# Second MLP's up-projections in seven products for eight, passes of 768 tokens, weights by way of DRAM; first MLP in 8+8 chunks

## The chip, the cores and the metric

One core of one Trainium2 chip. The metric is the device time of one execution in microseconds (us); lower is better. The time of the kernel before is the median of three runs. Executions differ by about 0.1% around it.

## The reference

A decayed linear attention on 2304 tokens (4 x 576), then two MLPs on its output. What matters here are the MLPs, with d_model 512:

```python
h = np.maximum(x @ w_in, 0.0)          # first MLP, d_ff 2048
x = h * h @ w_out
a, b = x @ w_a, x @ w_b                # second MLP, d_ff 1536
out = a * b @ w_out2
```

Inputs are float32 here; the weights arrive as float64 (pairs of 32-bit words) and are turned into float32 on the chip.

## The kernel before, in words

All matmuls of the MLPs work on float32 values split in two: a high part rounded to `fp32r` (ACT cast) and the remainder (DVE subtraction, `sub`, L236). A product is three matmuls: high weight x high data, low weight x high data, high weight x low data. `mm` (L227) issues each of them, so all matmuls of the kernel have that one line in the trace; the tiles tell them apart: `bank<-x,w` is an up-projection, `bank<-gh,w` a down-projection, `qkr`, `pt`, `tv` belong to attention.

The 2304 tokens are four `BLOCKS` of 512 and one of 256. d_ff is cut into chunks of 128: 16 in the first MLP, 12 in the second. `GROUPS` says which chunks are taken together: for each group all five blocks are run, and the group's sums over its chunks lie in banks 0 to 3 until the group's last chunk (`evac_y` L643 then copies or adds them to `yt` or `xt` in SBUF). `up(i)` (L670) issues one chunk and block: for each of `ph` weights (1 in the first MLP, 2 in the second) 4 x 3 matmuls into one of the `hbanks` (bank 7 alone until attention is over, then banks 4 to 7), then the element-wise step: Relu (L699) and Square (L713) on ACT in the first group, a copy (L699) and a product on DVE (L704, L708) in the others; then the split into `gh`. `down(i)` (L724) issues its 4 x 3 matmuls, written after the next chunk's `up`. `split_x` (L618) splits a block's input into four `x` slots.

A weight piece (512 columns) is loaded by `w_load` (L323): a transfer of 512 KB of float64 words into a `raw` buffer, ACT operations (L344, L370), four DVE operations (L348, L355, L363, L374) that put the float32 together in a `wf` buffer, then the split into a slot `w` of `wslot` by an ACT cast and a DVE subtraction. `pump` (L386) does that when a slot comes free. The first 16 pieces are loaded during attention. When attention and its buffers are done, `enter` (L761) gives their space to `yt`, three raw buffers and three more slots.

Nothing runs in the written order as such: every step goes to `Plan.add` with its engines, its cost and the buffers it reads and writes; `Plan.order` (L101) gives each step a latest start, taken back from the sequence of PE's work, and then plays through the engines, each taking the ready step with the earliest latest start. The order it finds is emitted, and each engine and the one transfer queue (SP) work it off in that order.

Of the kernel before, what the change touches and what calls it, by code (L numbers as in the profile page):

```python
# [44 lines left out]
WF, WE, RAWS = 4, 2, 3  # L45
SLOTS = dict(
    x=4, g=2, r=2, gh=2, qkr=3, vr=3, tv=2, pt=2, sa=2, wraw=4, ys=4,
# [162 lines left out]
def tile_retention_two_mlps(  # L210
# [36 lines left out]
    big = ctx.enter_context(tc.tile_pool(name="big", bufs=1))  # L247
    dram = ctx.enter_context(tc.tile_pool(name="dram", bufs=1, space=bass.MemoryType.DRAM))
    psum = ctx.enter_context(tc.tile_pool(name="psum", bufs=1, space=PSUM))

    xt = [big.tile([P, KT, n], F32, name=f"xt{t}") for t, (_, n) in enumerate(BLOCKS)]
# [16 lines left out]
    ring(big, "x", [P, 2, 512], F32R, SLOTS["x"])  # L268
# [3 lines left out]
    wslot = [big.tile([P, 2, 512], F32R, name=f"w{i}") for i in range(NW0)] + [None] * (NW - NW0)  # L272
# [4 lines left out]
    ap = st.enter_context(tc.tile_pool(name="attn", bufs=1))  # L277
# [28 lines left out]
    todo = [(ph, c, j) for ph, g in GROUPS for c in g for j in range(ph + 1)]  # L306
    wt = {}
    used = {}
    state_ = {"next": 0, "n": NW0, "entered": None, "loads": 0}
    raws = []  # L310

# [11 lines left out]
    def w_load(ph, c, j, i):  # L323

        w, kw = slot("wf")
        rest, ke = slot("we")
        src = (w1 if ph == 1 else w2)[c, :, j, :]
        parts = [("w", i, 0), ("w", i, 1)]
        ex = [state_["entered"]] if i >= NW0 else []
        wu = w.bitcast(U32)  # L330
# [12 lines left out]
        plan.add(  # L343
            {"ACT": act(512)}, lambda e: A.activation(w, hi().bitcast(F32), AF.Abs), [kraw], [kw]  # L344
        )
        plan.add(
            {"DVE": dve2(512)},
            lambda e: V.tensor_scalar(  # L348
                out=w, in0=w, scalar1=F64_MIN, scalar2=F64_MAX, op0=ALU.max, op1=ALU.min
            ),  # L350
            w=[kw],
        )
        plan.add(
            {"DVE": dve2(512)},
            lambda e: V.tensor_scalar(  # L355
                out=wu, in0=wu, scalar1=3, scalar2=0x3FFFFFF8,
                op0=ALU.logical_shift_left, op1=ALU.bitwise_and,
            ),
            w=[kw],
        )  # L360
        plan.add(
            {"DVE": dve(512)},
            lambda e: V.scalar_tensor_tensor(  # L363
                out=wu, in0=hi(), scalar=0xC0000000, in1=wu, op0=ALU.bitwise_and, op1=ALU.bitwise_or
            ),
            [kraw], [kw],
        )
# [4 lines left out]
        plan.add(  # L372
            {"DVE": dve(512)},
            lambda e: V._custom_dve(  # L374
                ADD32_U16LIMBS, out=w.bitcast(U16), in0=w.bitcast(U16), in1=rest.bitcast(U16)
            ),
            [ke], [kw],
        )
        plan.add({"ACT": act(512)}, copy(lambda: wslot[i][:, 0, :], lambda: w), [kw], parts[:1], ex)
        plan.add(  # L380
            {"DVE": dve(512), "POOL": pool(512)},
            sub(lambda: wslot[i][:, 1, :], lambda: w, lambda: wslot[i][:, 0, :]),
            [kw, parts[0]], parts[1:], ex,
        )

    def pump():  # L386
        while todo:
            i = state_["next"] % state_["n"]
            if i in used.values():
                return  # L390
            used[todo[0]] = i
            wt[todo[0]] = i
            state_["next"] = i + 1
            w_load(*todo.pop(0), i)
# [243 lines left out]
    for gi, (ph, g) in enumerate(GROUPS):  # L638
        for bi, t in enumerate(ORDERS[gi]):
            for ci, c in enumerate(g):  # L640
                seq.append((gi, ph, t, c, ci == 0, ci == len(g) - 1, bi == len(BLOCKS) - 1))

    def evac_y(gi, t, m):  # L643
        c0, n = BLOCKS[t]
        ph = GROUPS[gi][0]
# [11 lines left out]
        kd = tokens("yt" if ph == 1 else "xt", m, c0, n)  # L657

        def d():
            return yt[0][:, m, c0:c0 + n] if ph == 1 else xt[t][:, m, :]  # L660

        ex = [state_["entered"]]
        if gi == 0 or ph == 2 and GROUPS[gi - 1][0] == 1:
# [3 lines left out]
        if gi == len(GROUPS) - 1:  # L667
            plan.add(dmac(P * 4 * n), dma(lambda: out[:, m, c0:c0 + n], d), kd)

    def up(i):  # L670
        gi, ph, t, c, first, last, lastb = seq[i]
# [6 lines left out]
        for j in range(ph):  # L678
            b = hbanks[0][hbanks[1] % len(hbanks[0])]
            hbanks[1] += 1  # L680
            o, ko = bank[b], ("bank", b)
            wi = wt[ph, c, j]
            for k in range(KT):
                x, kx = xs[gi, t, k]

                def f(e, k=k, x=x, wi=wi, o=o):
                    w = wslot[wi]
                    cs = slice(k * P, (k + 1) * P)
                    mm(o[:, :n], w[:, 0, cs], x[:, 0, :n], k == 0, False)
                    mm(o[:, :n], w[:, 1, cs], x[:, 0, :n], False, False)  # L690
                    mm(o[:, :n], w[:, 0, cs], x[:, 1, :n], False, k == KT - 1)

                plan.add(mmc(n, n, n), f, [("w", wi, 0), ("w", wi, 1), kx, kx + (1,)], [ko])
                yield t
            if j == 0:
                fn = AF.Relu if ph == 1 else AF.Copy
                plan.add(
                    {"ACT": act(n, True)},
                    lambda e, o=o: A.activation(r[:, :n], o[:, :n], fn), [ko], [kr],  # L699
                )  # L700

        def prod(e):
            if ph == 1:
                V.scalar_tensor_tensor(  # L704
                    out=g[:, :n], in0=o[:, :n], scalar=0.0, in1=r[:, :n], op0=ALU.max, op1=ALU.mult
                )
            else:
                V.tensor_mul(g[:, :n], o[:, :n], r[:, :n])  # L708

        if gi == 0:  # L710

            for to, key in ((lambda: gh[:, 0, :n], kgh), (lambda: g[:, :n], kg)):
                plan.add({"ACT": act(n)}, lambda e, to=to: A.activation(to(), r[:, :n], AF.Square), [kr], [key])  # L713
        else:
            plan.add({"DVE": dve(n)}, prod, [ko, kr], [kg])
            plan.add({"ACT": act(n)}, copy(lambda: gh[:, 0, :n], lambda: g[:, :n]), [kg], [kgh])
        plan.add(
            {"DVE": dve(n), "POOL": pool(n)},
            sub(lambda: gh[:, 1, :n], lambda: g[:, :n], lambda: gh[:, 0, :n]),
            [kg, kgh], [kgh + (1,)],  # L720
        )
        return gh, kgh

    def down(i, gh, kgh):  # L724
        gi, ph, t, c, first, last, lastb = seq[i]
        n = BLOCKS[t][1]
        wi = wt[ph, c, ph]

        def f(e, ms, which):
            for m in ms:  # L730
                a, w, cs = bank[m][:, :n], wslot[wi], slice(m * P, (m + 1) * P)
                if 0 in which:
                    mm(a, w[:, 0, cs], gh[:, 0, :n], first, False)
# [5 lines left out]
        if last:  # L739
            for m in range(KT):  # L740
# [4 lines left out]
                evac_y(gi, t, m)  # L745
                yield t
        else:
            for h in range(2):
                for m in range(KT):
# [4 lines left out]
                    if m % 2 or h == 0:  # L754
                        yield t
        if lastb:
            for j in range(ph + 1):
                used.pop((ph, c, j))
            pump()

    def enter():  # L761
# [3 lines left out]
        def swap(e):  # L765
            st.close()
            late = ctx.enter_context(tc.tile_pool(name="late", bufs=1))
            yt[0] = late.tile([P, KT, NT], F32, name="yt")
            raws.extend(late.tile([P, 1024], U32, name=f"raw{i}") for i in range(RAWS))
            for i in range(NW0, NW):  # L770
                wslot[i] = late.tile([P, 2, 512], F32R, name=f"w{i}")
# [10 lines left out]
        state_["n"] = NW  # L782
        state_["next"] = NW0
        pump()

    rings_a = ["qkr", "vr", "tv", "pt", "wraw", "vt", "gt", "mask", "md", "sp", "sa", "ys"]

    def mlps():
        prev = None
        for i in range(len(seq)):  # L790
            gi, ph, t, c, first, last, lastb = seq[i]
# [9 lines left out]
        yield from down(len(seq) - 1, *prev)  # L801

# [6 lines left out]
    for t in mlps():  # L809
# [5 lines left out]
        before = plan.pe  # L815
    steps, total = plan.order()
# [72 lines left out]
```

## Time and profile before

| | |
|---|---|
| median of three runs | 907.05 us (906.63 to 907.87) |
| span of the profiled execution | 906.5 us |
| PE, PEld, DVE, ACT busy | 98%, 83%, 54%, 42% of the span |
| bytes moved | 66.12 MB, mean 73 GB/s |

The profile is of one execution, whose own time is not listed apart from the span; the span runs from its first to its last instruction. PE is TensorE's matmuls, PEld its weight loads, DVE is VectorE, ACT ScalarE, SP the engine that issues transfers. Matmuls overlap, so the time from the start of one group to the start of another tells more than a single duration. DVE and ACT durations contain an end that overlaps the next instruction.

### The profile page before, as it was taken

The page shows a single profiled execution, that of the slowest core. Times are in us where ns is not written, and L with a number is a line of the kernel's source. Part 1 is how long each engine was busy: PE and PEld are TensorE (multiplying, and loading weights), DVE is VectorE, ACT ScalarE, POOL GpSimd, SP SyncE. Part 2 cuts the span into 40 slices and gives each one's busy share as a digit, 9 for nine tenths or more (in the row PEclk, how much of TensorE's full clock was granted, in tenths as well). Part 3 has the DMA queues.
Part 4 walks back from the last instruction along what each step waited for, and adds up shares of the span by engine and source line. Part 5 has one row for each costly group of instructions (what it writes and reads, how often), then busy time and mean ns, then how long its engine had stood idle before and what let it go on. Part 6 is the DMA issues. An engine that isn't in the chain of part 4 may idle for free.

```text
span 906.5 us, 14973 instructions
## 1 busy us (share of the span) xinstructions
PE 891.6 (98%) x6256; PEld 755.4 (83%) x6256; DVE 492.1 (54%) x978; ACT 381.6 (42%) x703; POOL 0.7 (0%) x6
## 2 busy tenths in 40 slices
PE   5999999999999999999999999999999999999998
PEld 5787888888998889888888888898888898888888
DVE  6999544137699747964595213299332253322323
ACT  3676334346786536643464223276222132221221
POOL 0000000000000000000000000000000000000000
PEclk9999999999999999999999999999999999999999
DMA  8884531027343300310032000034000000011101
GB/s 271 296 275 123 177 105 48 1 56 259 129 138 106 103 1 24 117 47 1 1 117 70 1 1 1 1 96 138 0 1 1 1 1 1 9 38 47 46 2 71
DMA packets 22100, 66.12 MB, mean 73 GB/s; under 512 B 2448, under 2 KB 3088, under 8 KB 22032
## 3 DMA queue, kind: packets, MB, share of 16 engines
q1 hardware_dynamic: 21888, 65.15, 22.1%
q8 instruction: 49, 0.80, 0.4%
q14 instruction: 19, 0.16, 0.1%
q10 hardware_dynamic: 144, 0.01, 0.0%
HBM read 57.28 MB, written 7.86 MB: 72 GB/s over the span
## 4 chain that ended last, share of the span: by engine, by line
PE 94%; DVE 4%; DMA 1%; issue 1%; ACT 0%; SPq 0%; DVEq 0%; ACTq 0%
PE bank L227 94%; DMA vr<-vk 1%; DVE wf L374 1%; DVE wf L363 1%; DVE w L236 1%; DMA vt<-vtab 0%; DVE pt L567 0%; DVE sa L589 0%; DVE wf L348 0%; DVE xt L552 0%; DVE wf L355 0%; DVE gh L236 0%; ACT tv L477 0%; DVE xt L239 0%; ACT r L699 0%
## 5 line engine op out<-in xcount | busy, mean ns | idle before, releaser
L227 PE MATMUL bank<-x,w 128*128 128x512 f32 (+1 forms) x2400 | 535.9, 369 | 1.8 <-ACT r L699 0.7
L227 PEld LDWEIGHTS bank<-x,w 128*128 128x128 f32 x2400 | 420.4, 188 | 78.0 <-ACT r L699 1.1
L227 PE MATMUL bank<-gh,w 128*128 128x512 f32 (+1 forms) x1680 | 386.8, 369 | 0.4 <-DVE w L236 0.4
L227 PEld LDWEIGHTS bank<-gh,w 128*128 128x128 f32 x1680 | 296.0, 189 | 54.1 <-DVE w L236 1.1
L699 ACT ACTIVATE r<-bank 128x512 f32<-128x512 f32 (+1 forms) x140 | 77.6, 555 | 320.4 <-PE bank L227 320.0
L708 DVE TENSOR_TENSOR g<-bank,r 128x512 f32<-128x512 f32 (+1 forms) x60 | 38.3, 638 | 180.2 <-PE bank L227 179.3
L236 DVE TENSOR_TENSOR gh<-g,gh 128x512 fp32r<-128x512 f32 (+1 forms) x140 | 88.9, 635 | 70.1 <-ACT g L713 45.2
L233 ACT CAST gh<-g 128x512 fp32r<-128x512 f32 (+1 forms) x100 | 58.0, 580 | 110.9 <-DVE g L708 94.7
L236 DVE TENSOR_TENSOR x<-yt,x 128x512 fp32r<-128x512 f32 (+1 forms) x60 | 36.0, 634 | 50.2 <-ACT x L233 50.1
L233 ACT CAST w<-wf 128x512 fp32r<-128x512 f32 x68 | 41.7, 618 | 22.3 <-DVE wf L374 19.6
L236 DVE TENSOR_TENSOR w<-wf,w 128x512 fp32r<-128x512 f32 x68 | 46.4, 686 | 8.5 <-ACT w L233 8.0
L374 DVE CUSTOM_DVE_ANT_0 wf<-wf,we 128x1024 uint16<-128x1024 uint16 x68 | 46.4, 685 | 0.5
L236 DVE TENSOR_TENSOR x<-xt,x 128x512 fp32r<-128x512 f32 (+1 forms) x60 | 37.2, 635 | 12.2 <-ACT x L233 9.2
L704 DVE SCALAR_TENSOR_TENSOR g<-bank,r 128x512 f32<-128x512 f32 (+1 forms) x40 | 25.4, 636 | 30.5 <-ACT r L699 30.2
L370 ACT ACTIVATE we<-raw 128x512 int32<-128x512 uint32 x52 | 34.7, 671 | 14.5 <-DVE wf L374 14.1
L233 ACT CAST x<-xt 128x512 fp32r<-128x512 f32 (+1 forms) x60 | 33.8, 577 | 15.8 <-PE bank L227 15.3
L344 ACT ACTIVATE wf<-raw 128x512 f32<-128x512 f32 x52 | 34.4, 671 | 5.7 <-DMA raw<-w 5.1
L233 ACT CAST x<-yt 128x512 fp32r<-128x512 f32 (+1 forms) x60 | 33.4, 577 | 4.9 <-PE bank L227 4.0
L363 DVE SCALAR_TENSOR_TENSOR wf<-raw,wf 128x512 uint32<-128x512 uint32 x52 | 35.3, 685 | 0.2
L348 DVE TENSOR_SCALAR wf<-wf 128x512 f32<-128x512 f32 x68 | 28.1, 421 | 3.2 <-ACT wf L344 2.6
L239 DVE TENSOR_TENSOR yt<-bank,yt 128x512 f32<-128x512 f32 (+1 forms) x40 | 23.3, 630 | 11.3 <-PE bank L227 11.3
L355 DVE TENSOR_SCALAR wf<-wf 128x512 uint32<-128x512 uint32 x68 | 28.1, 421 | 0.2
(42 smaller groups left out, 367.9 us busy)
## 6 DMA issues: line engine op xcount, KB each, us to landing
raw<-w SPq DMA_DIRECT2D x52, 512.0 KB, 3.7
vr<-vk SPq DMA_DIRECT2D x16, 448.0 KB, 4.2
qkr<-qk SPq DMA_DIRECT2D x16, 448.0 KB, 4.8
wraw<-w SPq DMA_DIRECT2D x12, 512.0 KB, 6.6
out<-xt SPq DMA_DIRECT2D x16, 256.0 KB, 2.1
y<-ys SPq DMA_DIRECT2D x12, 256.0 KB, 2.5
yt<-y SPq DMA_DIRECT2D x3, 1024.0 KB, 8.1
qkr<-qk SPq DMA_DIRECT2D x4, 512.0 KB, 5.1
```

Of the source, the lines that this page charges most:

```text
L227: T.matmul(o, l, r, start=start, stop=stop, skip_group_check=True)
L233: return lambda e: A.copy(o(), i()) if e == "ACT" else eng[e].tensor_copy(o(), i())
L236: return lambda e: eng[e].tensor_sub(o(), a(), b())
L344: {"ACT": act(512)}, lambda e: A.activation(w, hi().bitcast(F32), AF.Abs), [kraw], [kw]
L348: lambda e: V.tensor_scalar(out=w, in0=w, scalar1=F64_MIN, scalar2=F64_MAX, op0=ALU.max, op1=ALU.min),
L355: lambda e: V.tensor_scalar(out=wu, in0=wu, scalar1=3, scalar2=0x3FFFFFF8, op0=ALU.logical_shift_left, op1=ALU.bitwise_and,),
L363: lambda e: V.scalar_tensor_tensor(out=wu, in0=hi(), scalar=0xC0000000, in1=wu, op0=ALU.bitwise_and, op1=ALU.bitwise_or),
L370: lambda e: A.activation(rest, lo(), AF.Copy, scale=LO_ULPS), [kraw], [ke],
L374: lambda e: V._custom_dve(ADD32_U16LIMBS, out=w.bitcast(U16), in0=w.bitcast(U16), in1=rest.bitcast(U16)),
L699: lambda e, o=o: A.activation(r[:, :n], o[:, :n], fn), [ko], [kr],
L704: V.scalar_tensor_tensor(out=g[:, :n], in0=o[:, :n], scalar=0.0, in1=r[:, :n], op0=ALU.max, op1=ALU.mult)
L708: V.tensor_mul(g[:, :n], o[:, :n], r[:, :n])
```

## The change

The second MLP is written anew in `second`. Its up-projections use Strassen's scheme in Winograd's form on 2 x 2 blocks: d_model in two halves, the weights `w_a` and `w_b` as the two block columns, and 2 x 384 tokens as the two block rows of x. A pass takes 768 tokens, so there are three passes; for each pass and chunk (a unit, 36 in all) seven products of two row blocks are formed in place of eight, 384 columns wide. The sums of x blocks are made in place in `yt` for each pass (`x_prep`: 7 splits and 4 combinations of 768 elements per partition) and held in seven operands `xo`, which take the place of `xt` and two x slots. Of the sums that join products, two are made by accumulating onto a bank: product 1 goes to the unit's bank 1, is copied by ACT to its bank 2, and product 3 adds onto bank 1; product 4 adds onto bank 2, which ACT then copies to bank 3; product 5 adds onto bank 2, product 6 onto bank 3, and after a DVE add has read bank 3, product 7 adds onto it. In the first unit on each set of banks, matmuls (`fresh`) open banks 2 and 3 (four in all). The down-projections have the same products as before, in pieces of two matmuls, and are mixed in behind the up products with a lag of five chunk-halves; their sums are evacuated five times in a pass.

Weights: after attention, the 16 remaining pieces of the first MLP and all 36 of the second are converted at once (`keep_first`, `keep_second`), the second MLP's combined (four DVE operations of 256), and stored in DRAM as float32; `fetch` loads a float32 piece (256 KB; one of the five of a chunk is 128 KB) straight into a slot's low half, and splits it there. Each pass fetches all 12 x 5 pieces of the second MLP again. Late raw buffers are two for three, slots 16 for 19. The first MLP runs in groups of 8 and 8 chunks for 8, 4 and 4, both with Relu and Square on ACT.

```diff
-GROUPS = [
-    (1, range(0, 8)), (1, range(8, 12)), (1, range(12, 16)),
-    (2, range(0, 4)), (2, range(4, 8)), (2, range(8, 12)),
-]
-ORDERS = [[0, 1, 2, 3, 4]] * 6
-NW0 = 2 * len(GROUPS[0][1])
-NW = 19
+GROUPS = [range(0, 8), range(8, 16)]
+ORDERS = [[0, 1, 2, 3, 4]] * 2
+NW = 16
+CH2 = 12
+N2 = 384
+PASSES = NT // (2 * N2)
+PIECES, OUTS = 8, 5
+RUN, LAG = 3, 5
 RATE = [0.35, 0.35, 0.35, 0.35, 0]
-WF, WE, RAWS = 4, 2, 3
+WF, WL, WE, RAWS = 4, 4, 2, 2
...
+    xb = [big.tile([P, 4, 512], F32R, name=f"xb{i}") for i in range(2)]
+    rings["x"] = [[xb[i // 2][:, 2 * (i % 2):2 * (i % 2) + 2, :] for i in range(4)], 0]
...
+    def split(to, kto, of, kof, n, ex=()):
+        plan.add({"ACT": act(n)}, copy(lambda: to()[:, 0, :n], of), [kof], [kto + (0,)], ex)
         plan.add(
-            {"DVE": dve(512), "POOL": pool(512)},
-            sub(lambda: wslot[i][:, 1, :], lambda: w, lambda: wslot[i][:, 0, :]),
-            [kw, parts[0]], parts[1:], ex,
+            {"DVE": dve(n), "POOL": pool(n)},
+            sub(lambda: to()[:, 1, :n], of, lambda: to()[:, 0, :n]),
+            [kof, kto + (0,)], [kto + (1,)], ex,
         )
+    def keep(name, of, kof, n):
+        kept[name] = dram.tile([P, n], F32, name="kept" + "_".join(map(str, name)))
+        plan.add(dmac(P * 4 * n), dma(lambda: kept[name], of), [kof], [("kept", name)])
+    def fetch(name, i, n):
+        h, l = ("w", i, 0), ("w", i, 1)
+        f = wslot[i].bitcast(F32)
+        plan.add(dmac(P * 4 * n), dma(lambda: f[:, 1, :n], lambda: kept[name]), [("kept", name)], [l])
+        plan.add({"ACT": act(n)}, copy(lambda: wslot[i][:, 0, :n], lambda: f[:, 1, :n]), [l], [h])
+        plan.add(
+            {"DVE": dve(n), "POOL": pool(n)},
+            sub(lambda: wslot[i][:, 1, :n], lambda: f[:, 1, :n], lambda: wslot[i][:, 0, :n]), [h], [l],
+        )
+    def keep_first():
+        for c, j in todo:
+            w, kw = w_float(w1[c, :, j, :])
+            keep((1, c, j), w, kw, 512)
+    def keep_second(c):
+        a, b, s = slice(0, 256), slice(256, 512), slice(0, 512)
+        wa, ka = w_float(w2[c, :, 0, :])
+        wb, kb = w_float(w2[c, :, 1, :])
+        keep((2, c, 0), wa, ka, 512)
+        ss, ks, exs = float_slot()
+        def op(fn, o, co, x, cx, y, cy, r, w):
+            plan.add(
+                {"DVE": dve(256)},
+                fn(lambda: o()[:, co], lambda: x()[:, cx], lambda: y()[:, cy]), r, w, exs,
+            )
+        op(sub, ss, b, wa, a, wb, a, [ka, kb], [ks])
+        op(add, wb, a, wb, a, wb, b, [], [kb])
+        op(sub, ss, a, wb, a, wa, a, [ka, kb], [ks])
+        op(sub, wa, b, wa, b, ss, a, [ks], [ka])
+        keep((2, c, 1), wb, kb, 512)
+        keep((2, c, 2), ss, ks, 512)
+        keep((2, c, 3), lambda: wa()[:, b], ka, 256)
+        wo, ko = w_float(w2[c, :, 2, :])
+        keep((2, c, 4), wo, ko, 512)
...
+        for to, key in ((lambda: gh[:, 0, :n], kgh), (lambda: g[:, :n], kg)):
+            plan.add({"ACT": act(n)}, lambda e, to=to: A.activation(to(), r[:, :n], AF.Square), [kr], [key])
...
+        keep_first()
+        for c in range(CH2):
+            keep_second(c)
...
+            def parts(o, i, j):
+                for k in xkeys[o]:
+                    plan.renew(k)
+                hk, lk = [k + (0,) for k in xkeys[o]], [k + (1,) for k in xkeys[o]]
+                plan.add(
+                    {"ACT": act(2 * n)}, copy(lambda: xo[o][:, 0], blk(i, j)), kb(i, j), hk, [swapped]
+                )
+                plan.add(
+                    {"DVE": dve(2 * n)}, sub(lambda: xo[o][:, 1], blk(i, j), lambda: xo[o][:, 0]),
+                    kb(i, j) + hk, lk, [swapped],
+                )
+            def comb(to, x, y):
+                plan.add({"DVE": dve(2 * n)}, sub(blk(*to), blk(*x), blk(*y)), kb(*x) + kb(*y), kb(*to))
+            parts(0, 0, 0)
+            comb((0, 0), (0, 1), (0, 0))
+            parts(1, 0, 0)
+            parts(2, 1, 0)
+            comb((0, 0), (1, 1), (0, 0))
+            parts(3, 0, 0)
+            parts(4, 1, 1)
+            comb((0, 1), (1, 1), (0, 1))
+            parts(5, 0, 1)
+            comb((1, 0), (1, 0), (0, 0))
+            parts(6, 1, 0)
+        pieces = {}
+        def piece(u):
+            for q in range(4):
+                i = turn["piece"] % PIECES
+                turn["piece"] += 1
+                pieces[u, q] = i
+                fetch((2, u % CH2, q), i, 256 if q == 3 else 512)
...
+        PRODUCTS = [
+            (0, 0, 0, 1, True), (1, 1, 0, 0, True), (2, 0, 256, 1, False), (3, 2, 0, 2, False),
+            (4, 3, 0, 2, False), (5, 2, 256, 3, False), (6, 1, 256, 3, False),
+        ]
+        def group(u, banks, fresh):
...
+            if fresh:
+                def f(e):
+                    for b in o[2:]:
+                        mm(b, wslot[pieces[u, 0]][:, 0, :P], xo[0][:, 0, 0], True, True)
+                w = pieces[u, 0]
+                plan.add(mmc(n, n), f, [("w", w, 0)] + [k + (0,) for k in xkeys[0]], ko[2:])
+            for i, (x, q, s, b, start) in enumerate(PRODUCTS):
+                w = pieces[u, q]
+                rd = [("w", w, 0), ("w", w, 1)] + [k + (h,) for k in xkeys[x] for h in range(2)]
+                for k in range(2):
+                    def f(e, x=x, w=w, s=s, b=b, k=k, start=start):
+                        cs = slice(s + k * P, s + k * P + P)
+                        mm(o[b], wslot[w][:, 0, cs], xo[x][:, 0, k], start and k == 0, False)
+                        mm(o[b], wslot[w][:, 1, cs], xo[x][:, 0, k], False, False)
+                        mm(o[b], wslot[w][:, 0, cs], xo[x][:, 1, k], False, k == 1)
+                    plan.add(mmc(n, n, n), f, rd, [ko[b]])
+                    yield
+                pa = {"ACT": act(n, True)}
+                if i == 0:
+                    plan.add(pa, copy(lambda: o[2], lambda: o[1]), [ko[1]], [ko[2]])
+                elif i == 1:
+                    p5, k5 = take_t()
+                    plan.add(pa, copy(p5, lambda: o[0]), [ko[0]], [k5])
+                elif i == 2:
+                    c11, k11 = take_t()
+                    plan.add(pa, copy(c11, lambda: o[1]), [ko[1]], [k11])
+                elif i == 3:
+                    plan.add(pa, copy(lambda: o[3], lambda: o[2]), [ko[2]], [ko[3]])
+                elif i == 4:
+                    c12, k12 = take_t()
+                    plan.add({"DVE": dve(n)}, add(c12, lambda: o[2], p5), [ko[2], k5], [k12])
+                elif i == 5:
+                    c22, k22 = take_t()
+                    plan.add({"DVE": dve(n)}, add(c22, lambda: o[3], p5), [ko[3], k5], [k22])
+                    plan.add({"DVE": dve(n)}, mul(c12, c12, c22), [k22], [k12])
+                else:
+                    plan.add({"DVE": dve(n)}, mul(c11, lambda: o[3], c11), [ko[3]], [k11])
+            for j, (g, kg) in enumerate(((c11, k11), (c12, k12))):
+                gh, kgh = take_g()
+                plan.add({"ACT": act(n)}, copy(lambda gh=gh: gh()[:, 0], g), [kg], [kgh + (0,)])
+                plan.add(
+                    {"DVE": dve(n), "POOL": pool(n)},
+                    sub(lambda gh=gh: gh()[:, 1], g, lambda gh=gh: gh()[:, 0]), [kg, kgh + (0,)], [kgh + (1,)],
+                )
+                made[p, j, c] = gh, kgh
...
+                if round_ == 0:
+                    plan.add({"ACT": act(n, True), "DVE": dve(n)}, copy(d, lambda: a[:, :n]), [ka], kd)
+                else:
+                    plan.add({"DVE": dve(n)}, add(d, lambda: a[:, :n], d), [ka], kd)
+                if c == CH2 - 1:
+                    plan.add(dmac(P * 4 * n), dma(lambda: out[:, m, c0:c0 + n], d), kd)
...
+        order, at, j, size = [], [0, 0], 0, RUN
+        while min(at) < CH2:
+            a, b = at[j], min(at[j] + size, CH2)
+            order += [(j, c, c == a, c == b - 1, int(a > 0)) for c in range(a, b)]
+            at[j], j, size = b, 1 - j, 2 * RUN
+        downs = (s for p in range(PASSES) for d in order for s in out_steps(p, *d))
+        rate = sum(4 if d[3] else 6 for d in order) / (14 * CH2)
+        due = -5.6 * LAG
+        x_prep(0)
+        piece(0)
+        for _ in range(OUTS):
+            out_piece()
+        piece(1)
+        for u in range(PASSES * CH2):
+            if u and u % CH2 == 0:
+                x_prep(u // CH2)
+            for _ in group(u, (0, 1, 2, 3) if u == 1 else (4, 5, 6, 7), u < 2):
+                due += rate
+                while due >= 1:
+                    next(downs)
+                    due -= 1
+            if u + 2 < PASSES * CH2:
+                piece(u + 2)
+        for _ in downs:
+            pass
```

## Rows read from the trace of the kernel before

**Rows 1.** The page: busy time of PE, DVE and ACT; PE and its clock by slices
```profile
PE 891.6 (98%) x6256; PEld 755.4 (83%) x6256; DVE 492.1 (54%) x978; ACT 381.6 (42%) x703; POOL 0.7 (0%) x6
...
PE   5999999999999999999999999999999999999998
...
PEclk9999999999999999999999999999999999999999
```

**Rows 2.** The chain that ended last: start us, length us, what
```profile
84.44 817.46 PE bank L227 x4826
```

**Rows 3.** Timeline of PE in a 512-token block, second MLP: start, length, line, operation
```profile
506.00 4.92 PE L227 MATMUL bank<-x,w 128*128 128x512 f32 x21
510.76 2.43 PE L227 MATMUL bank<-gh,w 128*128 128x512 f32 x10
513.02 0.84 PE L227 MATMUL bank<-x,w 128*128 128x512 f32 x3
...
514.16 4.92 PE L227 MATMUL bank<-x,w 128*128 128x512 f32 x21
```

**Rows 4.** The same in a 256-token block; first and last of 36 matmuls' four groups
```profile
743.31 1.12 PE L227 MATMUL bank<-gh,w 128*128 128x256 f32 x8
...
747.63 1.12 PE L227 MATMUL bank<-gh,w 128*128 128x256 f32 x8
```

**Rows 5.** Timeline of PE where the second MLP begins, and its last group
```profile
457.10 0.86 PE L227 MATMUL bank<-x,w 128*128 128x512 f32 x3
...
464.83 0.52 PE L227 MATMUL bank<-gh,w 128*128 128x256 f32 x3
...
899.86 3.10 PE L227 MATMUL bank<-gh,w 128*128 128x256 f32 x24
```

**Rows 6.** Timeline in the first MLP, where up-projections have bank 7 alone
```profile
165.96 2.20 PE L227 MATMUL bank<-x,w 128*128 128x512 f32 x9
...
168.00 2.43 PE L227 MATMUL bank<-gh,w 128*128 128x512 f32 x10
168.20 0.60 ACT L699 ACTIVATE r<-bank 128x512 f32<-128x512 f32 x1 [3.65 <-PE bank L227]
...
170.26 0.84 PE L227 MATMUL bank<-x,w 128*128 128x512 f32 x3
```

**Rows 7.** Groups of instructions by form: count, busy us, mean ns of one
```profile
L236 DVE TENSOR_TENSOR gh<-g,gh 128x512 fp32r<-128x512 f32 x112 | 77.2, 689 | 67.9 <-ACT g L713 45.0 <-ACT gh L233 22.6
...
L699 ACT ACTIVATE r<-bank 128x512 f32<-128x512 f32 x112 | 67.0, 598 | 284.3 <-PE bank L227 283.9
...
L374 DVE CUSTOM_DVE_ANT_0 wf<-wf,we 128x1024 uint16<-128x1024 uint16 x68 | 46.4, 685 | 0.5
...
L348 DVE TENSOR_SCALAR wf<-wf 128x512 f32<-128x512 f32 x68 | 28.1, 421 | 3.2 <-ACT wf L344 2.6
...
L236 DVE TENSOR_TENSOR gh<-g,gh 128x256 fp32r<-128x256 f32 x28 | 11.8, 420 | 2.2 <-ACT gh L233 1.9 <-ACT g L713 0.2
L699 ACT ACTIVATE r<-bank 128x256 f32<-128x256 f32 x28 | 10.7, 380 | 36.2 <-PE bank L227 36.1
```

**Rows 8.** Windows of 20 us: busy time of each engine, clock, DMA share, GB/s
```profile
20.00:40.00 20.00, 16.88 (x300) 14.32 (x303) 18.51 (x48) 13.19 (x26) 0.00 (x0) 0.91 0.88 307
...
280.00:300.00 20.00, 20.00 (x90) 16.58 (x89) 19.30 (x37) 12.20 (x23) 0.00 (x0) 1.00 0.38 116
```

**Rows 9.** SP's issues of late loads: count, issue ns (min/median/max), first and last start
```profile
L242 SPq DMA_DIRECT2D raw<-w x52: 327/328/425, 201.7 to 631.2; - x52
```

**Rows 10.** Transfers by their issues: count, KB each, median us to landing
```profile
raw<-w SPq DMA_DIRECT2D x52, 512.0 KB, 3.7
...
out<-xt SPq DMA_DIRECT2D x16, 256.0 KB, 2.1
...
out<-xt SPq DMA_DIRECT2D x4, 128.0 KB, 1.8
```

**Rows 11.** Timeline of DVE, four subtractions in a row
```profile
258.32 2.50 DVE L236 TENSOR_TENSOR x<-xt,x 128x512 fp32r<-128x512 f32 x4
```

More of the change, by code (lines that the diff above doesn't have):

```diff
@@ L276, in tile_retention_two_mlps @@
     st = ExitStack()
-    ap = st.enter_context(tc.tile_pool(name="attn", bufs=1))
+    ap = st.enter_context(tc.tile_pool(name="attn", bufs=1, side="right"))
     most = max(LONG, NP * (S // C - LONG))
@@ L303, in tokens @@
         return [(name, k, j) for j in range(c0 // 32, (c0 + n) // 32)]
-    todo = [(ph, c, j) for ph, g in GROUPS for c in g for j in range(ph + 1)]
+    todo = [(c, j) for g in GROUPS for c in g for j in range(2)]
+    early = todo[:NW]
     wt = {}
     used = {}
-    state_ = {"next": 0, "n": NW0, "entered": None, "loads": 0}
+    state_ = {"next": 0, "entered": None, "loads": 0, "floats": 0}
     raws = []
+    kept = {}
     def raw_slot():
@@ L666, in evac_y, with halves @@
             plan.add({"DVE": dve(n)}, add(d, lambda: a[:, :n], d), [ka], kd, ex)
-        if gi == len(GROUPS) - 1:
-            plan.add(dmac(P * 4 * n), dma(lambda: out[:, m, c0:c0 + n], d), kd)
+    def halves(gh, kgh, g, kg, n):
+        plan.add(
+            {"DVE": dve(n), "POOL": pool(n)},
+            sub(lambda: gh[:, 1, :n], lambda: g[:, :n], lambda: gh[:, 0, :n]),
+            [kg, kgh], [kgh + (1,)],
+        )
     def up(i):
-        gi, ph, t, c, first, last, lastb = seq[i]
+        gi, t, c, first, last, lastb = seq[i]
         n = BLOCKS[t][1]
@@ L677, in up @@
         gh, kgh = slot("gh")
[L678 to L716, printed above, removed]
+        b = hbanks[0][hbanks[1] % len(hbanks[0])]
@@ new lines, in up, with f @@
+        hbanks[1] += 1
+        o, ko = bank[b], ("bank", b)
+        wi = wt[c, 0]
+        for k in range(KT):
+            x, kx = xs[gi, t, k]
+            def f(e, k=k, x=x, wi=wi, o=o):
+                w = wslot[wi]
+                cs = slice(k * P, (k + 1) * P)
+                mm(o[:, :n], w[:, 0, cs], x[:, 0, :n], k == 0, False)
+                mm(o[:, :n], w[:, 1, cs], x[:, 0, :n], False, False)
+                mm(o[:, :n], w[:, 0, cs], x[:, 1, :n], False, k == KT - 1)
+            plan.add(mmc(n, n, n), f, [("w", wi, 0), ("w", wi, 1), kx, kx + (1,)], [ko])
+            yield t
@@ L722, in up, with down_steps @@
+        halves(gh, kgh, g, kg, n)
         return gh, kgh
[L724 to L727, printed above, removed]
+    def down_steps(wi, gh, kgh, n, start, last, evac):
         def f(e, ms, which):
@@ L732, in f @@
                 if 0 in which:
-                    mm(a, w[:, 0, cs], gh[:, 0, :n], first, False)
+                    mm(a, w[:, 0, cs], gh[:, 0, :n], start, False)
                     mm(a, w[:, 1, cs], gh[:, 0, :n], False, False)
@@ L754, in down @@
                     if m % 2 or h == 0:
-                        yield t
+                        yield
+    def down(i, gh, kgh):
+        gi, t, c, first, last, lastb = seq[i]
+        n = BLOCKS[t][1]
+        for _ in down_steps(wt[c, 1], gh, kgh, n, first, last, lambda m: evac_y(gi, t, m)):
+            yield t
         if lastb:
-            for j in range(ph + 1):
-                used.pop((ph, c, j))
+            for j in range(2):
+                used.pop((c, j))
             pump()
@@ L766, in swap @@
             st.close()
-            late = ctx.enter_context(tc.tile_pool(name="late", bufs=1))
+            late = ctx.enter_context(tc.tile_pool(name="late", bufs=1, side="right"))
             yt[0] = late.tile([P, KT, NT], F32, name="yt")
             raws.extend(late.tile([P, 1024], U32, name=f"raw{i}") for i in range(RAWS))
-            for i in range(NW0, NW):
-                wslot[i] = late.tile([P, 2, 512], F32R, name=f"w{i}")
+            floats.extend(late.tile([P, 512], F32, name=f"wl{i}") for i in range(WL))
+            tmp.extend(late.tile([P, N2], F32, name=f"tmp{i}") for i in range(4))
+            tmp.append(late.tile([P, 2, N2], F32R, name="ghl"))
         state_["entered"] = plan.add({}, swap, extra=deps)
@@ L790, in mlps @@
         for i in range(len(seq)):
-            gi, ph, t, c, first, last, lastb = seq[i]
+            gi, t, c, first, last, lastb = seq[i]
             if gi == 0 and first:
@@ L815, in tile_retention_two_mlps @@
         before = plan.pe
+    second()
     steps, total = plan.order()
```

176 lines of the change are left out of this document (140 added, 36 removed).

## The prediction

> **What bounds the kernel now.** I read the page's busy lines and slices first: PE is busy 98% of the span, DVE 54%, ACT 42%, and from the second slice on PE stands at 9 at full granted clock [rows 1]. The chain that ended last says the same in order of time: one piece of 817.46 us that holds PE alone, from 84.44 to 901.9, behind which only the last evacuation and its stores lie [rows 2]. So after 84 us only the sum of the matmuls counts, as long as nothing makes PE wait.
>
> A busy PE could still be a slow one, so next come the spacings. In the second MLP one chunk of a 512-token block is 36 matmuls; the first one of a chunk starts at 506.00 and that of the next at 514.16 [rows 3]: 8.16 / 36 = 0.22667 us. In a 256-token block the same 36 go from 743.31 to 747.63 [rows 4]: 4.32 / 36 = 0.1200 us. At 2.4 GHz 512 columns take 213.33 ns and 256 take 106.67, so both rows leave 13.33 ns per matmul, whatever its width. With these the second MLP adds up: 12 chunks x 36 x (4 x 0.22667 + 0.1200) = 443.5 us. Its first matmuls start at 457.10, with 16 matmuls of the first MLP (4, 9 and 3 in three groups, 0.12 each, 1.9 us) still to come; 457.1 + 443.5 + 1.9 = 902.5, and the last group ends at 899.86 + 3.10 = 902.96 [rows 5]. At most 0.4 us of waiting is in it.
>
> **The change: matmuls.** A unit (chunk x pass of 768 tokens) issues 7 products x 2 row blocks x 3 = 42 up matmuls and 2 x 4 x 3 = 24 down matmuls, 66, all of 384 columns. Three passes of 12 chunks make 36 units, 2376 matmuls for 2160. Columns fall from 995,328 to 912,384. No row has 384 columns; the line through the two measured widths gives 160 + 13.33 = 173.33 ns. (Their own ratios would give 170.0 and 180.0, but neither has the same fixed part at both widths; I let the fixed part be wrong by 1 ns either way, 2.4 us.) After: 2376 x 0.17333 = 411.8 us. Removed: 443.5 - 411.8 = **31.7 us**. Four opening matmuls in the first two units cost 4 x 0.173 = 0.7 back. The first MLP has the same matmuls in 8+8 chunks as in 8+4+4, and attention is untouched: 0. The stretch up to 84 us, where PE does wait for DVE, still loads the same 16 weight pieces through the same buffers: 0.
>
> The Trainium skill gives a smaller fixed part: "TensorE: Matmul & The Clock Gate", section "Back-to-back issue gap", has N / 2.4 + 2.5 ns. By it the second MLP would go from 420.1 to 386.1, 34.0 saved; the trace shows 13.33 at both widths, and the measurement decides.
>
> **The change: turnarounds in PSUM.** This is where it can go wrong. Before, a finished bank is read once and taken later by another product. Now product 4 is copied by ACT from bank 2 to bank 3, and product 5 adds onto bank 2 right after; product 6's bank 3 is read by a DVE add and product 7 adds onto it. Product 3 adds onto bank 1 after a copy too, but product 2 (six matmuls, 1.04 us) lies between. Price of one turnaround: ACT starts 0.04 us after the ninth matmul's end (165.96 + 2.20, to 168.20) and takes 0.60 for 512 columns [rows 6], 0.38 for 256 [rows 7], so 0.49 for 384 (below 0.38 or above 0.60 it can't well be, a PSUM destination being unseen); with some 0.1 for the way back, my estimate, 0.63. The DVE add, 0.69 and 0.42, gives 0.555 and 0.69 in all. Uncovered, 1.32 us a unit, 36 x 1.32 = 47.5 us. The cover is 24 down matmuls a unit (4.2 us) of chunks made two to three units earlier, which depend on neither bank. In the written sequence about 0.8 of a two-matmul piece (0.28 us) falls into each gap, which would leave 0.35 + 0.41 = 0.76 a unit, 27 us. But PE's order is not the written one: the planner takes what is ready. The rows show it: the source issues 24 up and then 12 down matmuls, the trace has 21 x, 10 gh, 3 x of the next chunk, and then the last 2 gh [rows 3]; and while one bank 7 was evacuated, ten gh matmuls were put between its last and next writer with no gap [rows 6]. I take 0 for it.
>
> The Trainium skill speaks against exactly this: "Perfetto Trace Analysis", section "Matmuls", asks that independent groups rotate through different PSUM banks so that evacuation overlaps the next group, and calls larger matmuls more efficient. By that the price would be the 27 to 47 above; the trace's single bank 7, reused at full rate, agrees that other work can stand in for rotation.
>
> **ACT and DVE in the second MLP.** A unit takes 66 x 0.173 = 11.4 us of PE. By durations [rows 7], 384 taken halfway: ACT has 4 PSUM copies (2.0), 2 casts (1.0) and 4 weight casts and a half one (taken as L699's, 2.8): 5.8. DVE has 6 operations of 384 (3.3), 4 weight subtractions and a half one (3.2), evacuations (20 of 384 a pass, 0.9) and the preparation of x (11 of 768, about 0.96 each, 10.5 a pass, 0.9): 8.3, 73%. Hidden: DVE was busy 19.3 of 20 us with PE full [rows 8]. Without that cover each us over 11.4 would cost 36.
>
> **Weights by way of DRAM.** After attention 52 pieces are converted, stored as float32 and fetched back. The first late load was issued at 201.7 [rows 9]; the second MLP starts near 459, so 257 us. DVE: conversions 52 x (0.685 + 0.421 + 0.421 + 0.685) = 115, combinations 48 x 0.42 = 20, splits of fetched pieces 19, the first MLP's own subtractions, x splits and evacuations 64, x of the first pass 10: 229, 89% by durations. Four in a row took 2.50 instead of 2.74 [rows 11], so nearer 80%. Raw buffers go from 3 to 2: a cycle is 3.7 to land [rows 10] plus 0.33 issue and one ACT and three DVE operations (0.6 + 0.42 + 0.42 + 0.685), 6.15, half of that per piece, 52 x 3.1 = 161 us, done near 365. Transfers: 27.3 MB raw, 18.4 stored, 7.3 fetched, 3.1 of y, 56 MB in 257 us, 218 GB/s; 307 was reached [rows 8]. SP issues them in one row, so a store that waits for DVE holds up the loads behind it; what is late then is a piece with some 90 us of slack, except the first-MLP pieces of chunks 8 to 15, ready by about 260 and due from 259 to 297 in turn. Cost 0; without the slack, each us of a late first piece is a us.
>
> **Boundaries and tail.** Each pass refills seven single-buffered x operands in step with the last unit that reads them: 10.5 us of DVE plus some 3.5 of exposed ACT, 14 us in chain, against about 10.4 us of backlogged down matmuls (28 pieces, 0.35 each) and the unit's own remaining products. Bounds 0 and 3.6 at each of three places; I take 0.5, 1.5 together. For the start there are 8 x 24 x 0.12 = 23 us of the last 256-block, more than 14. Tail: the last add is 384 wide for 256 (0.13) and the last store 192 KB between 1.8 and 2.1 us [rows 10]: 0.3.
>
> **Sum.** The profiled execution's span is 906.5 us, 0.55 below the median of 907.05. 906.5 - 31.7 + 0.7 + 1.5 + 0.3 = 877.3; with the 0.55, **878 us**.
>
> **Rivals.**
> A, the other side: the two turnarounds are not covered. 907 - 31 + 27 = 903 with the written order, 907 - 31 + 47.5 = 923.5 with none; it decides against the change from 31 / 36 = 0.86 us a unit, two thirds of the full price. Against it: the pulled-forward matmuls above. For it: two reuses of one bank inside each unit, where before there was none so close. 8 in 100, of which 6 end above 909.
> B: the x refill at the boundaries and DVE at the edges of the stages: 3 x 3.6 = 10.8, 882 to 889. For it: DVE needs about 23 us in the 20 around a boundary (10.5 plus 1.75 units of 7.4 without the x). Against it: weight subtractions can be put off a unit. 20 in 100.
> C: the DRAM detour is late: DVE at 89% and 218 GB/s through one queue, PE waits 11 to 24 us between 200 and 470: 889 to 902. Against it: full PE beside a DVE at 96%. 9 in 100.
> D: the skill's fixed part, or any smaller one at 384: 874 to 875.5. 2 in 100.
> My forecast, 875.5 to 882, has 61.
>
> **Range and chances.** 875.5 to 889 holds the forecast and B, 81 in 100. A measurement tells about 0.2% (1.8 us) from no change. Faster: all but the worst of A, 0.93; same 0.01; slower 0.06.
>
> **What would show it.** Right: 2376 matmuls of 384 columns, 66 in 11.44 us in the middle of a pass; PE at 9 in every slice after the fourth; DVE near 73% in the second MLP. Turnarounds: PE idle ended by the ACT copy or by the DVE add, repeated 36 times. Boundaries: PE idle before the first products of passes 2 and 3, ended by the x subtraction. The detour: idle near 260 or 460 ended by a weight split or a load. The prediction is wrong if the matmuls of 384 stand at another spacing than 173 ns, or if any of these waits is more than 2 us in all.

## The result, and the profile after

The changed kernel takes 877.81 us (median of 4, 876.58 to 880.17), the one before, measured with it, 907.46. The ratio is 0.9671, 95% interval 0.965 to 0.9692. Forecast were 878.0 us and a range of 875.5 to 889.

The page of the changed kernel: busy time, and two rows of the slices, which answer to [rows 1].

```profile
PE 861.3 (98%) x6476; PEld 791.5 (90%) x6476; DVE 575.7 (66%) x1149; ACT 484.7 (55%) x934; POOL 0.7 (0%) x6
...
PE   6899999999999999999999999999999999999998
...
PEclk9999999999999999999999999999999999999999
```

The chain that ended last, changed kernel, start us, length us, what; it answers to [rows 2].

```profile
84.24 787.08 PE bank L228 x5046
```

PE alone is still the chain from 84 us on, at full clock; DVE went from 54% to 66%, ACT from 42% to 55%, and nothing came of it on PE. The piece is 30.4 us shorter than before. (Matmuls are now L228, since the file has other lines.)

The timeline of PE in the changed kernel: a stretch in the middle of a pass, then the first matmuls of the second MLP, the last group but one of the first, and the last group of all.

```profile
530.42 0.51 PE L228 MATMUL bank<-w,w 128*128 128x384 f32 x2
530.77 0.68 PE L228 MATMUL bank<-xo,w 128*128 128x384 f32 x3
531.29 0.51 PE L228 MATMUL bank<-w,w 128*128 128x384 f32 x2
```
```profile
457.26 2.07 PE L228 MATMUL bank<-xo,w 128*128 128x384 f32 x11
459.17 1.59 PE L228 MATMUL bank<-gh,w 128*128 128x256 f32 x12
...
870.62 2.25 PE L228 MATMUL bank<-xb,w 128*128 128x384 f32 x12
```

Five matmuls take 0.87 us from start to start, 0.174 each, where the line through the two widths before had 0.1733 (the tile names differ because `gh` parts lie in slots `w`, in `xb` and in `ghl`). The second MLP begins 0.16 us later than in [rows 5]. From there 2380 matmuls of 0.1733 and twelve of 0.12 make 414.0 us, which would end at 871.2; they end at 870.62 + 2.25, of which 0.16 is drain: 872.7. So 1.5 us of waiting are in it, in pieces of 0.15 us and less.

Windows of the changed kernel, columns as in [rows 8]: the second MLP, the stretch with the detour through DRAM, and the boundary of the first two passes.

```profile
455.00:870.00 415.00, 415.00 (x2398) 413.88 (x2397) 249.09 (x447) 213.68 (x428) 0.00 (x0) 1.00 0.36 106
200.00:457.00 257.00, 257.00 (x1309) 220.36 (x1308) 205.41 (x392) 174.99 (x331) 0.00 (x0) 1.00 0.71 220
580.00:600.00 20.00, 20.00 (x117) 20.00 (x116) 19.98 (x34) 13.30 (x25) 0.00 (x0) 1.00 0.42 125
```

PE is full in all three. DVE has 60% of the second MLP, 80% of the detour, and at the boundary 19.98 of 20 us.

### The profile page after: what moved, and what is told of

Read it like the earlier page. It is cut to its first block, busy times and chain, and to the rows that moved or that the text cites. A ratio compares the mean times of both kernels' runs of the same rounds, so it can differ in the third digit from the quotient of the medians.

```text
span 876.4 us, 16597 instructions
## 1 busy us (share of the span) xinstructions
PE 861.3 (98%) x6476; PEld 791.5 (90%) x6476; DVE 575.7 (66%) x1149; ACT 484.7 (55%) x934; POOL 0.7 (0%) x6
## 4 chain that ended last, share of the span: by engine, by line
PE 94%; DVE 4%; DMA 1%; issue 1%; ACT 1%; SPq 0%; DVEq 0%; ACTq 0%
PE bank L228 94%; DVE wf L393 1%; DVE wf L382 1%; DMA vr<-vk 1%; DVE w L237 0%; DMA vt<-vtab 0%; DVE sa L664 0%; DVE pt L642 0%; DVE wf L374 0%; DVE wf L367 0%; DVE yt L240 0%; DVE gh L237 0%; DVE xt L627 0%; ACT tv L552 0%; ACT r L774 0%
## 5 line engine op out<-in xcount | busy, mean ns | idle before, releaser
L228 PE MATMUL bank<-xb,w 128*128 128x512 f32 (+2 forms) x1392 | 314.6, 359 | 1.6 <-ACT r L774 0.7
L228 PEld LDWEIGHTS bank<-xb,w 128*128 128x128 f32 x1392 | 244.3, 188 | 34.2 <-ACT r L774 1.1
L228 PE MATMUL bank<-gh,w 128*128 128x512 f32 (+2 forms) x1188 | 273.9, 362 | 0.4 <-DVE w L237 0.4
L228 PE MATMUL bank<-xo,w 128*128 128x384 f32 x1300 | 267.5, 334 | 0.0
L228 PEld LDWEIGHTS bank<-gh,w 128*128 128x128 f32 x1188 | 209.5, 188 | 31.2 <-DVE w L237 1.1
L228 PEld LDWEIGHTS bank<-xo,w 128*128 128x128 f32 x1300 | 229.1, 188 | 0.0
L237 DVE TENSOR_TENSOR w<-w 128x512 fp32r<-128x512 f32 (+1 forms) x196 | 124.0, 637 | 36.3 <-ACT w L234 34.9
L234 ACT CAST w<-w 128x512 fp32r<-128x512 f32 (+1 forms) x196 | 113.0, 580 | 54.6 <-DMA w<-kept 47.5
L228 PE MATMUL bank<-w,w 128*128 128x384 f32 x312 | 71.6, 334 | 0.0
L228 PEld LDWEIGHTS bank<-w,w 128*128 128x128 f32 x312 | 55.7, 188 | 0.0
L240 DVE TENSOR_TENSOR yt<-bank,yt 128x384 f32<-128x384 f32 (+2 forms) x56 | 31.6, 582 | 10.4 <-PE bank L228 10.2
```

The costliest lines, as they stand in the source:

```text
L228: T.matmul(o, l, r, start=start, stop=stop, skip_group_check=True)
L234: return lambda e: A.copy(o(), i()) if e == "ACT" else eng[e].tensor_copy(o(), i())
L237: return lambda e: eng[e].tensor_sub(o(), a(), b())
L240: return lambda e: eng[e].tensor_add(o(), a(), b())
```

## The experiments

**The regrouping alone.** The kernel before with the first MLP in 8+8 chunks.

```diff
-    (1, range(0, 8)), (1, range(8, 12)), (1, range(12, 16)),
+    (1, range(0, 8)), (1, range(8, 16)),
...
-ORDERS = [[0, 1, 2, 3, 4]] * 6
+ORDERS = [[0, 1, 2, 3, 4]] * 5
```

> The kernel before with one edit: the first MLP in groups of 8 and 8 chunks. Theory of the prediction (PE's matmuls alone set the time): the matmuls are the same, so 907.4, within 1 us. Rival (the regrouping, with one round of evacuations and x splits less, gives part of the 30 us): below 900.

Measured: 907.16 us beside 907.35; ratio 0.9998 (0.9987 to 1.0009). One round of evacuations and of x splits less gives nothing that could be told: PE's matmuls are the same.

**Eight products, all else kept.** The changed kernel with plain products. The sums of weights are still made, stored and fetched, and `wb` is stored before it is summed; the sums of x, the copies between banks and the opening matmuls are left out, as nothing needs them.

```diff
-            (0, 0, 0, 1, True), (1, 1, 0, 0, True), (2, 0, 256, 1, False), (3, 2, 0, 2, False),
-            (4, 3, 0, 2, False), (5, 2, 256, 3, False), (6, 1, 256, 3, False),
...
+        PRODUCTS = [(0, 0, 1), (0, 1, 0), (1, 0, 2), (1, 1, 3)]
...
+            for i, (j, q, b) in enumerate(PRODUCTS):
+                w = pieces[u, q]
+                for h in range(2):
+                    x = 2 * j + h
...
-        rate = sum(4 if d[3] else 6 for d in order) / (14 * CH2)
+        rate = sum(4 if d[3] else 6 for d in order) / (16 * CH2)
```

> The changed kernel with eight plain products for seven: same passes of 768, same stores and fetches through DRAM, same down-projections; four x operands and no sums of x, no copies between banks, no opening matmuls. Theory of the prediction: 2592 matmuls of 384 columns for 2380, 212 x 0.17333 = 36.7 us more, 914.5 (913 to 917), slower than the kernel before by what 384 columns cost against 512 (some 7). Rival (passes, the DRAM detour or the new mixing give the gain, not the seventh product): 890 or less.

Measured: 913.88 us (912.98 to 914.56); ratio to the kernel before 1.0059 (1.0041 to 1.0077). It is 36.1 us behind the changed kernel, where 212 matmuls of 0.1733 make 36.7. So the gain comes from seven products in place of eight, and passes, detour and narrower matmuls alone are a loss of some 6.5 us: 13.33 ns for each of 432 matmuls more than before is 5.8.

**PE in written order.** Each matmul step of the second MLP waits for the one written before it.

```diff
+        if "PE" in engines:
+            if self.chain:
+                deps.add(self.last)
+            self.last = n
...
+        plan.chain = True
         x_prep(0)
```

> The changed kernel with PE held to the written order in the second MLP (each matmul step waits for the one written before it; nothing else changes). Theory of the prediction (the two turnarounds of a unit cost nothing only because other matmuls are put into them): 0.76 us a unit come open, 27 us, 905 (895 to 912). Rival (the turnarounds are too short to matter): 878 to 882.

Measured: 924.84 us, ratio to the kernel before 1.0182 (1.0153 to 1.0211). 47.0 us above the changed kernel: more than both theories said. Not all of it lies in the second MLP. The edit moved the planner's order ahead of it too: attention's last matmuls run at 199 us, for 150 in the changed kernel, and the second MLP begins late:

```profile
463.14 4.67 PE L233 MATMUL bank<-xo,w 128*128 128x384 f32 x26
```

That is 5.9 us after the 457.26 of the changed kernel, so some 41 of the 47.0 us are the second MLP's, 1.14 a unit.

**Written order, and nothing in the gaps.**

```diff
             for _ in group(u, (0, 1, 2, 3) if u == 1 else (4, 5, 6, 7), u < 2):
                 due += rate
-                while due >= 1:
-                    next(downs)
-                    due -= 1
+            while due >= 1:
+                next(downs)
+                due -= 1
```

> As the run in written order, and the down pieces of a unit written behind its seven products, so that nothing lies in the gaps. Theory of the prediction: the full price of 1.32 us a unit, 47.5 us, 925 (915 to 932). Rival (the turnarounds are too short to matter): 878 to 885.

Measured: 946.63 us, ratio to the kernel before 1.0422 (1.0392 to 1.0452), 68.8 us above the changed kernel, 1.91 a unit where 1.32 were forecast. Who waited for whom on PE in the second MLP of this kernel (us in total, times, longest):

```profile
PE bank L233 <- ACT bank L239: 20.0, 36, 0.7
PE bank L233 <- DVE tmp L245: 13.1, 18, 0.7
PE bank L233 <- DVE g L245: 12.7, 18, 0.7
```

Its timeline around one unit's two gaps: PE, its weight loads, and the two operations in between:

```profile
571.71 1.73 PE L233 MATMUL bank<-xo,w 128*128 128x384 f32 x9
573.99 2.35 PE L233 MATMUL bank<-xo,w 128*128 128x384 f32 x12 [0.55 <-ACT bank L239]
577.08 1.14 PE L233 MATMUL bank<-xb,w 128*128 128x384 f32 x5 [0.74 <-DVE tmp L245]
```
```profile
573.99 2.03 PEld L233 LDWEIGHTS bank<-xo,w 128*128 128x128 f32 x12 [0.87 <-ACT bank L239]
```
```profile
573.47 0.46 ACT L239 COPY bank<-bank 128x384 f32<-128x384 f32 x1 [0.51 <-PE bank L233]
...
576.48 0.55 DVE L245 TENSOR_TENSOR tmp<-bank,tmp 128x384 f32<-128x384 f32 x1
```

The copy between banks behind product 4 and the add behind product 6 each stand in the way 36 times. Here PE is idle 0.55 us for the copy, where the prediction had 0.63, and 0.74 for the add, where it had 0.69: 1.29 for its 1.32. The view of waits gives 45.8 us over 36 units, 1.27 a unit. The other 20 us it does not count. They are in the rows: the group before the gap ends at 571.71 + 1.73 = 573.44, 0.16 later than the next matmul would have started in a stream (a matmul lasts 0.334 and the next one starts after 0.173); and the twelve matmuls behind the gap take 2.35, where twelve without a gap take 2.24:

```profile
862.23 2.24 PE L228 MATMUL bank<-w,w 128*128 128x384 f32 x12
```

(a row of the changed kernel). The weight loads, too, begin again only at 573.99, with the first of these matmuls. So the copy's gap costs 0.55 + 0.16 + 0.11 = 0.82 and the add's 0.74 + 0.27 = 1.01, together 1.83 a unit and 66 us. The second MLP of this run begins at 459.81, 2.5 us later than in the changed kernel: 68.5, against the 68.8 measured. In written order, 1.83 - 1.14 = 0.69 a unit is covered, two down matmuls (0.35) in each gap on average, where the prediction had 0.28.

**Each fetch transferred twice.**

```diff
+        if name[0] == 2:
+            plan.add(dmac(P * 4 * n), dma(lambda: f[:, 1, :n], lambda: kept[name]), [("kept", name)], [l])
```

> The changed kernel with each fetch of a second-MLP piece transferred twice into the same slot (42 MB more read). Theory of the prediction (the detour through DRAM is hidden, a piece has a unit of slack): 878, within 1.5 us. Rival (transfers or SP's one queue are near their limit in the second MLP): 882 or more, with PE waiting for weight splits.

Measured: 878.63 us (877.05 to 880.91), against 877.81. The window of its second MLP, 205 GB/s for 106, and PE full:

```profile
455.00:870.00 415.00, 414.79 (x2398) 413.06 (x2398) 258.36 (x455) 214.05 (x431) 0.00 (x0) 1.00 0.67 205
```

**One late raw buffer.**

```diff
-WF, WL, WE, RAWS = 4, 4, 2, 2
+WF, WL, WE, RAWS = 4, 4, 2, 1
```

> The changed kernel with one late raw buffer for two, so that half as many late loads are under way. Theory of the prediction (a buffer's cycle of some 6 to 7 us sets the pace of the late conversions): the 16 first-MLP pieces take 98 to 112 us, the last pair is ready near 306 to 320 and due at 297, so PE waits 9 to 23 us in the first MLP and nowhere else: 887 to 901. Rival (the conversions have slack to spare even so): 878 to 880.

Measured: 896.76 us, 18.9 above the changed kernel. Its timeline of PE in the first MLP's second group, and SP's issues of raw loads (times and durations as in [rows 9]):

```profile
297.09 0.51 PE L228 MATMUL bank<-gh,w 128*128 128x512 f32 x1 [3.76 <-ACT w L234]
297.81 4.37 PE L228 MATMUL bank<-gh,w 128*128 128x512 f32 x11 [0.22 <-DVE w L237]
303.48 0.50 PE L228 MATMUL bank<-xb,w 128*128 128x512 f32 x1 [1.29 <-ACT w L234]
...
310.96 0.49 PE L228 MATMUL bank<-gh,w 128*128 128x512 f32 x1 [2.38 <-ACT w L234]
...
317.15 0.51 PE L228 MATMUL bank<-xb,w 128*128 128x512 f32 x1 [1.06 <-ACT w L234]
```
```profile
L246 SPq DMA_DIRECT2D raw<-w x52: 327/333/1082, 199.3 to 590.1; - x52
```

PE waits for the splits of first-MLP pieces, there and hardly anywhere else, as forecast. The four long waits are 8.5 us of the 18.9. Behind the first of them eleven matmuls take 4.37 us, where [rows 3] make it 2.66 (ten take 2.43, one more 0.23): the granted clock was no longer full, and the window around it has 0.79 (columns as in [rows 8]).

```profile
300.00:320.00 20.00, 14.49 (x41) 9.97 (x40) 10.10 (x17) 7.95 (x14) 0.00 (x0) 0.79 0.54 158
```

Part of this stretch ran at the lower of the clock's two levels, 1.2 GHz, after PE had waited 3.76 us. The groups of eleven behind the waits at 303.48 and 310.96 take 4.38 and 4.31 us. At 1.7 us each these are some 5 us that the theory did not have. A load comes every (590.1 - 199.3) / 51 = 7.7 us, and the last of them, in the second MLP, still cost next to nothing.

**More DVE work in a unit.** Each half's remainder is written four times, or seven times, for once.

```diff
+                for _ in range(4):
                     plan.add(
                         {"DVE": dve(n), "POOL": pool(n)},
                         sub(lambda gh=gh: gh()[:, 1], g, lambda gh=gh: gh()[:, 0]), [kg, kgh + (0,)], [kgh + (1,)],
                     )
```

> The changed kernel with six more DVE subtractions of 384 in each unit of the second MLP (each half's remainder written four times over). DVE's load of a unit by time from start to start: 6.9 + 6 x 0.47 = 9.7 of 11.44, 878 to 881. By the durations that the prediction summed: 8.3 + 6 x 0.555 = 11.6 of 11.44, over the limit, 884 or more.

> The same with twelve more subtractions a unit. By time from start to start: 6.9 + 12 x 0.47 = 12.5 of 11.44, 36 x 1.1 = 38 us more, 916 (908 to 922). By durations: 8.3 + 12 x 0.555 = 15.0, 127 us more, 1005.

Measured: 877.74 us with six more (877.18 to 878.14), 909.19 with twelve (907.08 to 911.55). The windows of their second MLPs, the six first:

```profile
455.00:870.00 415.00, 415.00 (x2394) 413.88 (x2393) 342.91 (x663) 212.57 (x425) 0.00 (x0) 1.00 0.35 106
```
```profile
455.00:900.00 445.00, 430.32 (x2411) 421.30 (x2410) 437.56 (x884) 213.24 (x426) 0.00 (x0) 0.98 0.33 99
```

83% of DVE leaves PE alone; with twelve DVE has 98% and is the bound, and 31.4 us more over 36 units make a unit of 12.3 us, where start to start gave 12.5 and durations 15.0. (The granted clock of that window is 0.98, so a part of the 31.4 may be the clock's; it was not told apart.) The load of DVE goes by starts. By (11.44 - 6.9) / 0.47 the changed kernel has room for some nine more such operations in a unit, an estimate, since only six and twelve were tried.

**Can the start be shortened?** First MLP in groups of 6, 6, 4, then 7, 5, 4 chunks.

```diff
-GROUPS = [range(0, 8), range(8, 16)]
-ORDERS = [[0, 1, 2, 3, 4]] * 2
+GROUPS = [range(0, 6), range(6, 12), range(12, 16)]
+ORDERS = [[0, 1, 2, 3, 4]] * 3
```

> The changed kernel with the first MLP in groups of 6, 6 and 4 chunks for 8 and 8; the same matmuls. Theory (PE's sum sets the time after 84 us, DVE's conversion of the first pieces before it): the first block needs 12 pieces for 16 before PE runs full, so up to 4 x 2.9 = 11.6 us of DVE move behind other work and the time falls by 2 to 8 us, to 870 to 876. Rival (PE's idle time before 84 us comes from attention's own waits, or the missing MLP work leaves it bare): 878 to 884, the same or slower.

> The same with groups of 7, 5 and 4 chunks. Theory: half the effect of 6, 6 and 4, 1 to 4 us less, 874 to 877. Rival: 878 to 881.

Measured: 876.84 (876.68 to 879.95) and 878.21 us (877.08 to 879.28): no change that could be told. The chain with 6, 6, 4:

```profile
67.60 802.56 PE bank L228 x5322
```

PE alone begins at 67.60 for 84.24, but the piece is 15.5 us longer. What PE got done before 84 us did not rise with it. The full-width matmuls up to there are 96 + 73 in the changed kernel and 96 + 78 here, the latter two rows being of this run (groups of instructions, up to 84 us):

```profile
L228 PE MATMUL bank<-xb,w 128*128 128x512 f32 x96 | 24.8, 395 | 2.5 <-ACT xb L234 1.3 <-ACT r L774 0.7 <-DVE xb L237 0.5
L228 PE MATMUL bank<-gh,w 128*128 128x512 f32 x78 | 21.4, 399 | 0.3 <-DVE w L237 0.3
```

Five more, 1.1 us. What holds PE there besides the conversions was not tried.

## Why the prediction was right

**Matmuls.** 31.7 - 0.7 saved by 2380 matmuls at 173.33 ns: the spacing, 174, is in the rows, and the eight-product run gives 36.1 for the 36.7 of the same arithmetic. This term carries the result; the regrouping gives 0. By the Trainium skill, page "TensorE: Matmul & The Clock Gate", section "Back-to-back issue gap", the estimate is 162.5 ns at 384; the measured 174 decides.

**Turnarounds.** The 0 was right and its reason is shown: with the order taken away the kernel loses. The timeline of PE and of ACT in the changed kernel around one copy between banks shows the cover:

```profile
533.71 1.37 PE L228 MATMUL bank<-xo,w 128*128 128x384 f32 x7
534.93 0.85 PE L228 MATMUL bank<-w,w 128*128 128x384 f32 x4
535.62 0.51 PE L228 MATMUL bank<-gh,w 128*128 128x384 f32 x2
535.97 1.20 PE L228 MATMUL bank<-xo,w 128*128 128x384 f32 x6
```
```profile
535.12 0.46 ACT L234 COPY bank<-bank 128x384 f32<-128x384 f32 x1 [0.51 <-PE bank L228]
```

Six down matmuls of two chunks stand between product 4 and product 5, 1.04 us, for a gap of 0.82. The price of rival A was too low: 27 and 47.5 us forecast, some 41 and 66 found in the second MLP (47.0 and 68.8 in all). The step that failed is the price itself, "0.63" and "0.69 in all": as idle time of PE the two were nearly right, 0.55 and 0.74, though their 0.1 for the way back rested on no row (0.05 to 0.06 in the rows above). They left out the exposed end of the last matmul and the slow start of the next, 0.27 a gap and 0.54 a unit. So rival A's bounds, 903 and 923.5, were measured as 924.84 and 946.63, and the written order alone turns the change into a loss of 1.8%, which the prediction had as a gain of 4 us. The forecast did not suffer, as it took 0.

**ACT and DVE.** ACT was forecast at 5.8 of 11.4 us a unit; 213.68 of 415 is 5.9. DVE was forecast at 73% and had 60%: the sum took durations, where each of some 13 operations a unit overlaps the next by 0.085 us (0.555 long, 0.47 from start to start), 1.1 us, and 24 of the 60 evacuations went to ACT, 0.4 us. The term was too large, on the safe side.

**Weights by way of DRAM.** DVE "nearer 80%" and 218 GB/s stand at 80% and 220. The pace was mis-sized. SP's raw loads and their landing in the changed kernel:

```profile
L246 SPq DMA_DIRECT2D raw<-w x52: 332/333/426, 201.4 to 421.4; - x52
```
```profile
raw<-w SPq DMA_DIRECT2D x52, 512.0 KB, 4.2
```

One load every 4.3 us, not 3.1, so done near 430 and not 365: a buffer's cycle is 8.6 us, as landing takes 4.2 and the buffer is then held until DVE has read it. What SP waited for between 200 and 425 us (us in total, times, longest; L382 is the DVE operation that reads the raw buffer):

```profile
SPq L246 <- DVE wf L382: 53.0, 25, 7.0
SPq L246 <- DVE wl L382: 34.1, 19, 5.5
```

The first-MLP pieces, which the prediction had ready by about 260, are split at 290.8 at the latest. The last of an up-projection, by their order, is split at 287.2 and first used at 296.5, so the slack was some 9 us there and not 37. The cost was 0 all the same. That the slack is finite, and lies in the first MLP's pieces, is what the run with one buffer shows; the first pieces of the second MLP had until 457.

**Boundaries and tail.** At the boundaries 1.5 us were forecast; in the window 580 to 600 PE is full beside a full DVE (and so it is from 720 to 740 at the next boundary, DVE 19.12), so rival B didn't come about, and the 1.5 us found in the second MLP are not there: in neither window does a matmul start more than 0.02 us late. They agree in size by chance. (The 10.4 us of backlog in the prediction are 28 pieces of 0.37, since 134 pieces hold 288 matmuls; by the 0.35 written there they would be 9.8.) The tail was forecast 0.3 longer; from the last matmul's end to the end of the span it is 876.4 - 872.9 = 3.5 us, as before (906.5 - 903.0).

**The sum.** Forecast span 877.3, measured 876.4; the profiled execution took 878.13 us, 1.7 more than its span, where 0.55 had been allowed. The 906.5 of before had likewise been one execution's span, set against a median of three runs. The two errors, 0.9 too much and 1.15 too little, cancel in the 878: that it came out within 0.2 us is luck, though the terms behind it are right to about 1 us.

## What to carry to other kernels

When PE sets the time, count columns and matmuls, take the spacing at two widths from the trace, and the line through them prices a third width to a fraction of a per cent; fewer products pay only where the work they bring fits under PE on other engines, and that load is summed from start to start, not by durations. A scheme that reads a bank and goes on adding to it opens gaps worth 0.8 and 1.0 us here, so price it with the end of the last matmul and the restart, and look first whether independent matmuls can be issued between: the same kernel is 3% faster with them and 4% slower without. A buffer count that looks generous is best tried at one less, which shows where its slack is; the waits that come of it can cost more than their length, as here, where the granted clock fell behind them.

## What was not expected of the hardware

A matmul stream of 384 columns that stopped for a bank lost 0.27 us beyond the idle time that the view of waits shows: 0.16 of exposed end and 0.11 in the matmuls behind the gap (2.35 for 2.24 us), whose weight loads began no sooner than they did. With one raw buffer, eleven matmuls took 4.37 us for 2.66 behind a wait of 3.76 us, at a granted clock of 0.79. And doubling the reads of the second MLP to 205 GB/s, with PE, ACT and DVE at work, did not move the time by more than a measurement tells.
